# A recurrent cross-attention block with a maxout FFN on one core: another order of the work, single PSUM banks, two batches scored with the states standing, and the last batch's output in fewer pieces

## The chip, the cores and the metric

The kernel runs on one core of a Trainium2 chip. A core has a matrix engine (TensorE, PE in the profile), a vector engine (VectorE, DVE), an activation engine (ScalarE, ACT), a general engine (GpSimd, POOL) and an engine that here only issues transfers (SyncE, SP). Each works through its own list of instructions in order; semaphores hold an instruction back until what it needs is there. The time is device microseconds of the whole program, the median of the runs shown. A profile of one execution gives the span, from its first to its last instruction.

## The reference, cut to what matters

```python
# x: (8, 8, 512, 64), state: (8, 8, 32, 64): batches, heads, tokens, head width
scores  = x @ state.T / 8;   a  = exp(scores - max) / sum      # over the 32 states
scores2 = state @ x.T / 8;   a2 = exp(scores2 - max) / sum     # over the 512 tokens
y = concat([a @ state, a2 @ x], axis=2)                        # 512 + 32 rows per batch and head
# heads side by side: 8 * 544 = 4352 rows of 512
h = max(y @ w1, y @ w2, y @ w3)                                # w: (512, 768)
out = h @ w_out                                                # (4352, 512), float32
```

## The kernel before, in words

The work is in bfloat16 with sums in float32. The kernel doesn't form `a @ state` for the tokens. It multiplies the states of each batch with w1, w2 and w3 first (G, `g_slice` and `g_run`: 64x32 blocks of states as weights, eight of them at a time in the array, since a batch has eight heads), and layer 1 is then one product of the turned weights `aT` with G (`layer1`, L477: six matmuls of 512 columns for each of the six 128-column blocks of the 768). The maximum of three is taken in three steps: ACT copies the first product out of PSUM (`max_first`, L492), VectorE takes the maximum with the second and the third (`max_second` L497, `max_third` L505). Layer 2 is six matmuls into one PSUM bank for each quarter of a batch's tokens (`layer2`, L514); ACT or VectorE copies it out (L526) and a DMA stores it. The 32 state rows of all batches are collected and go through both layers once, at the end (`layer1_states`, `s` in the lists below). The last batch's layer 2 is done in column pieces (`layer2_part` L532, `layer2_part_out` L537, `store_part` L543).

Per batch, ahead of layer 1: the states are cast and turned (`states_cast`, `states_turn` with the matrix engine, four transposes; `states_turn_dma` with a DMA), x is turned (by DMA from batch 2 on), the scores are made (`scores`, L305: 16 matmuls with x as weights and the states' blocks as 64 moving columns), ACT takes the exponential (`exps`, L313), VectorE sums (L342), GpSimd multiplies by the reciprocals (`weights`, L349), and the result is turned by DMA (`a_turn_dma`, L366). `scores_turned`, `exps_turned` and `e_turn_dma`, which stand in the code but not in the order of before, are the other way round: the states' blocks are the weights, x moves, and the exponentials are turned by DMA. The state rows' reading (`sread`, L391) uses the exponentials and x with a column of ones (`pad`).

PSUM has eight banks. Before, four are used singly (tags b0 to b3) and four as two pairs (w0, w1); G and the scores go to pairs, so that one copy takes two banks at once. BANKS, PAIRS and PLACES say which bank or buffer each use takes, in order.

The order of everything is written out by hand: PLAN is a list of short words with arguments, and each word calls one function (`lw 0 2 1`: load columns 0 to 256 of w2; `g 0 1`: G of batch 0, block 1; `l1 3 5`; `l2 2 0`; `so 2 0 2 P`: store from GpSimd's queue). Each engine gets its instructions in the order of that list. In the list of before, batches 3 to 6 repeat one pattern.

The exponentials are taken without subtracting the maximum. `look` takes the largest and smallest of all sums, `flag` (`set_flag`, L575 to L578) makes one number of it with a small matmul and two VectorE instructions, and `vl` (L583) has all five engines read that number. A branch (L674) leads to a second path, which does everything again with the maximum subtracted; with these inputs it is skipped. `hold` puts one matmul and one copy (L591, L593) ahead of the reads. Behind the branch each engine passes some semaphores and a barrier that closes the program (L739).

Of the kernel before, what the change touches and what calls it, by code (L numbers as in the profile page):

```python
# [13 lines left out]
ALU = mybir.AluOpType  # L14
# [4 lines left out]
    lst 0 A; lxu 0 0 S; zero; clr 0; clr 1; clr 2; clr 3; warm; lxg 0 1; busy 1; xones 1; ident; busy 1;  # L19
    lxg 1 0; busy 1; busy 1; stc 0 D; busy 1; busy 1; busy 1; busy 1; busy 1; lxg 1 1; stt 0; busy 1; busy 1;  # L20
    cxu 0 0 D; xt 0 0; stp 0 A; busy 1; xt 0 1; lw 0 2 1; lw 0 1 0; xtc 0 0 D; sc 0 0; xones 0; lw 0 2 2;
    xtc 0 1 D; busy 1; busy 1; sc 0 1; xt 1 0; ex 0 0; ex 0 1; lw 1 3 0; sum 0 0; sum 0 1; xtc 1 0 A; busy 1;
    busy 1; xt 1 1; sc 1 0; xtc 1 1 D; ex 1 0; busy 1; busy 1; sc 1 1; lw 2 3 2; wt 0 1 D; lw 2 3 1; lw 3 4 0;
    wt 0 0 P; lw 3 6 2; at 0 0; sr 0; ex 1 1; sr 1; g 0 0; sum 1 0; wt 1 0 P; g 1 0; atc 0 0 A; at 0 1; at 1 0;
    gc 0 0 A; atc 0 1 A; g 1 1; sum 1 1; gc 1 0 D; atc 1 0 A; srs 0; srs 1; g 0 1; wt 1 1 P; at 1 1; gc 0 1 A;
    l1 0 0; atc 1 1 D; lst 1 A; m0 0 0; lst 3 A; gc 1 1 A; ma 0 0; lw 3 6 1; lw 4 6 0; lxg 2 1; lxg 2 0; l1 0 1;
    m0 0 1; lwo; mb 0 0; g 0 2; g 1 2; ma 0 1; l1 1 0; lst 2 A; gc 0 2 A; mb 0 1; m0 1 0; ma 1 0; l1 0 2;
    mb 1 0; gc 1 2 A; m0 0 2; ma 0 2; l1 1 1; m0 1 1; g 1 3; stc 1 P; mb 0 2; ma 1 1; g 0 3; mb 1 1; stt 1;
    gc 1 3 A; l1 1 2; gc 0 3 A; m0 1 2; stp 1 DA; ma 1 2; g 0 4; g 0 5; l1 0 3; gc 0 5 D; g 1 4; mb 1 2;
    gc 0 4 A; m0 0 3; gc 1 4 A; ma 0 3; gr 2 1792 2304; mb 0 3; l1 1 3; m0 1 3; grc 2 1792 2304 A; xtd 2;  # L30
    ma 1 3; l1 0 5; stc 2 P; g 1 5; gr 2 0 512; mb 1 3; m0 0 5; ma 0 5; l1 1 4; gc 1 5 A; gr 2 1280 1792;
    m0 1 4; grc 2 0 512 D; mb 0 5; gr 2 512 1024; ma 1 4; grc 2 1280 1792 AD; l1 0 4; m0 0 4; ma 0 4; stt 2;
    mb 0 4; sc 2 -; ex 2 -; grc 2 512 1024 D; stp 2 AD; stc 3 D; mb 1 4; l2 0 3; l2 0 0; l2c 0 3 A; l2c 0 0 A;
    sum 2 -; l2 0 1; ones; pad 2; lxg 3 0; lxg 3 1; wt 2 - P; stt 3; xtd 3; l2c 0 1 A; l1 1 5; pad 3;
    so 0 0 2 P; lx 4; m0 1 5; l2 0 2; ma 1 5; mb 1 5; stp 3 A; l2c 0 2 A; l2 1 0; gq 2 1024 1280; gr 3 0 512;
    gr 3 1792 2304; l2c 1 0 D; grc 3 1792 2304 D; gqc 2 1024 1280 A; grc 3 0 512 A; atd 2; sr 2; l2 1 1; srs 2;
    sc 3 -; l1 2 0; m0 2 0; ex 3 -; l2c 1 1 D; l2 1 3; ma 2 0; gq 3 1024 1280; so 0 2 4 P; gqc 3 1024 1280 A;
    l2c 1 3 A; gr 3 512 1024; gr 3 1280 1792; mb 2 0; sum 3 -; wt 3 - P; atd 3; xtd 4; srt 0; sr 3; srs 3;
    l1 2 1; m0 2 1; ma 2 1; l1 2 2; m0 2 2; mb 2 1; ma 2 2; l1 2 3; m0 2 3; mb 2 2; ma 2 3; l1 2 5; m0 2 5;
    mb 2 3; l2 1 2; grc 3 1280 1792 A; grc 3 512 1024 A; ma 2 5; mb 2 5; l2c 1 2 D; l1 2 4; so 1 2 4 P; m0 2 4;  # L40
    ma 2 4; lx 5; mb 2 4; so 1 0 2 P; pad 4; gr 4 1792 2304; gr 4 0 512; grc 4 1792 2304 AD; l2 2 0; l2 2 1;
    grc 4 0 512 D; l2c 2 0 A; l1 3 0; m0 3 0; sc 4 -; ex 4 -; xtd 5; l2c 2 1 D; l2 2 3; ma 3 0; gq 4 1024 1280;
    gr 4 1280 1792; gr 4 512 1024; mb 3 0; sr 4; gqc 4 1024 1280 A; sum 4 -; srs 4; l2c 2 3 A; l1 3 1; m0 3 1;
    ma 3 1; l1 3 2; m0 3 2; mb 3 1; ma 3 2; l1 3 3; m0 3 3; mb 3 2; ma 3 3; l1 3 5; wt 4 - P; m0 3 5; mb 3 3;
    l2 2 2; grc 4 1280 1792 A; grc 4 512 1024 A; ma 3 5; mb 3 5; l2c 2 2 D; l1 3 4; so 2 2 4 P; m0 3 4; ma 3 4;
    lx 6; mb 3 4; atd 4; srt 1; ap 0 A; so 2 0 2 P; pad 5; gr 5 1792 2304; gr 5 0 512; grc 5 1792 2304 AD;
    l2 3 0; l2 3 1; grc 5 0 512 D; l2c 3 0 A; l1 4 0; m0 4 0; sc 5 -; ex 5 -; xtd 6; l2c 3 1 D; l2 3 3; ma 4 0;
    gq 5 1024 1280; gr 5 1280 1792; gr 5 512 1024; mb 4 0; sr 5; gqc 5 1024 1280 A; sum 5 -; srs 5; l2c 3 3 A;
    l1 4 1; m0 4 1; ma 4 1; l1 4 2; m0 4 2; mb 4 1; ma 4 2; l1 4 3; m0 4 3; mb 4 2; ma 4 3; l1 4 5; wt 5 - P;
    m0 4 5; mb 4 3; l2 3 2; grc 5 1280 1792 A; grc 5 512 1024 A; ma 4 5; mb 4 5; l2c 3 2 D; l1 4 4; so 3 2 4 P;  # L50
    m0 4 4; ma 4 4; lx 7; mb 4 4; atd 5; srt 2; ap 1 A; so 3 0 2 P; pad 6; gr 6 1792 2304; gr 6 0 512;
    grc 6 1792 2304 AD; l2 4 0; l2 4 1; grc 6 0 512 D; l2c 4 0 A; l1 5 0; m0 5 0; sc 6 -; ex 6 -; xtd 7;
    l2c 4 1 D; l2 4 3; ma 5 0; gq 6 1024 1280; gr 6 1280 1792; gr 6 512 1024; mb 5 0; sr 6; gqc 6 1024 1280 A;
    sum 6 -; srs 6; l2c 4 3 A; l1 5 1; m0 5 1; ma 5 1; l1 5 2; m0 5 2; mb 5 1; ma 5 2; l1 5 3; m0 5 3; mb 5 2;
    ma 5 3; l1 5 5; wt 6 - P; m0 5 5; mb 5 3; l2 4 2; grc 6 1280 1792 A; grc 6 512 1024 A; ma 5 5; mb 5 5;
    l2c 4 2 D; l1 5 4; so 4 2 4 P; m0 5 4; ma 5 4; mb 5 4; atd 6; srt 3; ap 2 A; so 4 0 2 P; pad 7;
    gr 7 1792 2304; gr 7 0 512; grc 7 1792 2304 AD; l2 5 0; l2 5 1; grc 7 0 512 D; l2c 5 0 A; l1 6 0; m0 6 0;
    sc 7 -; ex 7 -; l2c 5 1 D; l2 5 3; ma 6 0; gq 7 1024 1280; gr 7 1280 1792; gr 7 512 1024; mb 6 0; sr 7;
    gqc 7 1024 1280 A; sum 7 -; srs 7; l2c 5 3 A; l1 6 1; m0 6 1; ma 6 1; l1 6 2; m0 6 2; mb 6 1; ma 6 2;
    l1 6 3; m0 6 3; mb 6 2; srt 4; ma 6 3; l1 6 5; wt 7 - P; m0 6 5; mb 6 3; l2 5 2; grc 7 1280 1792 A;  # L60
    grc 7 512 1024 A; ma 6 5; mb 6 5; l2c 5 2 D; l1 6 4; so 5 2 4 P; m0 6 4; ma 6 4; mb 6 4; atd 7; ap 3 A;
    ap 4 A; so 5 0 2 P; srt 6; l1 7 0; srt 7; m0 7 0; l2 6 0; ap 7 D; srt 5; ma 7 0; mb 7 0; l1 7 2; m0 7 2;
    ap 6 A; l2c 6 0 D; ma 7 2; l1 7 3; m0 7 3; ap 5 A; mb 7 2; ma 7 3; l1 7 4; m0 7 4; l2 6 1; l2c 6 1 A;
    ma 7 4; mb 7 4; l1s 0; m0 s 0; l2 6 2; l2c 6 2 A; look; ma s 0; mb s 0; so 6 2 3 S; mb 7 3; l1 7 1; m0 7 1;
    ma 7 1; l1s 2; m0 s 2; mb 7 1; ma s 2; l1 7 5; m0 7 5; mb s 2; ma 7 5; l1s 1; m0 s 1; ma s 1; so 6 0 1 S;
    mb 7 5; l1s 5; m0 s 5; l2p 7 2 384 512; ma s 5; mb s 1; mb s 5; l1s 3; m0 s 3; l2pc 7 2 384 512 A;
    l2p 7 0 384 512; l2p 7 3 256 512; sop 7 2 384 512 P; ma s 3; l2p 7 2 128 384; mb s 3; l2p 7 0 0 128;
# [38 lines left out]
def kernel(  # L106
# [74 lines left out]
    def bank(shape, dtype, name):  # L181
        return pp.tile(shape, dtype, tag="b" + next(homes["b"]), bufs=1, name=name)
# [491 lines left out]
    with tc.If(bad != 0, label="again"):  # L674
        for b in range(B):
# [11 lines left out]
            if b >= 2:  # L687
                pad(b)
# [55 lines left out]
```

## Time and profile before

| | |
|---|---|
| device time, median of 3 runs | 152.12 us (152.12 to 152.29) |
| span of the profiled execution | 150.5 us |
| granted TensorE clock | 1.000 |
| TensorE busy | 145.1 us, 96% of the span, 1422 matmuls |
| VectorE, ACT, GpSimd busy | 118.0, 83.2, 56.1 us |
| DMA | 22.29 MB, mean 148 GB/s |

The profiled execution has its span; no device time of its own is recorded beside it, so it is set against the runs shown, which are 1.62 us longer at the median. Busy times are unions of instructions that overlap: a 512-column matmul is shown with 379 ns, but six of them follow each other in 1.29 us. Which engine sets the time is therefore read from the chain of work that ended last, and from the idle time ahead of groups of instructions. "L477" is line 477 of the kernel before.

### The profile page before, as it was taken

Reading aid. Unit: us, or ns where it says so; the run is one execution under the profiler, and the core shown is the slowest. Engines: PE = TensorE matmul, PEld = TensorE weight load, DVE = VectorE, ACT = ScalarE, POOL = GpSimd, SP = SyncE. Lnnn points to the kernel's source line nnn. Section 1 sums busy time; section 2 is a strip of 40 time slices with the busy share of each in tenths; the row PEclk is TensorE's granted clock in tenths of the full one; section 3 lists DMA queues with packets and bytes.
Section 4 is the critical chain, followed back from the end, with each engine's and each line's share of the span. In section 5 each row is a group of like instructions: output and inputs, shape, how many; then the busy total and the mean of one; then the engine's idle time right before and its main releaser. Section 6 shows DMA issues by size and latency. Waiting matters only on the chain.

```text
span 150.5 us, 3618 instructions
## 1 busy us (share of the span) xinstructions
PE 145.1 (96%) x1422; PEld 72.8 (48%) x1422; DVE 118.0 (78%) x202; ACT 83.2 (55%) x144; POOL 56.1 (37%) x78
## 2 busy tenths in 40 slices
PE   6998999999999999999999999999999999999991
PEld 2556443335444443444344434443444446689770
DVE  6488788999967899789978997899789888674443
ACT  3366888965654574457546764676466653332220
POOL 6996911090392507350735064506250200001500
PEclk9999999999999999999999999999999999999999
DMA  4999999949647996998399839983303340300555
GB/s 121 195 188 189 206 230 198 196 97 139 124 97 171 235 182 189 108 209 178 145 102 216 183 139 90 231 183 131 157 4 78 121 175 7 139 0 17 190 199 167
DMA packets 39108, 22.29 MB, mean 148 GB/s; under 512 B 23072, under 2 KB 36896, under 8 KB 39088
## 3 DMA queue, kind: packets, MB, share of 16 engines
q0 software_dynamic: 15872, 13.96, 49.3%
q1 hardware_dynamic: 21632, 6.69, 22.8%
q10 hardware_dynamic: 1584, 1.38, 3.2%
q8 instruction: 12, 0.20, 0.6%
q14 instruction: 8, 0.07, 0.2%
HBM read 15.20 MB, written 8.91 MB: 160 GB/s over the span
## 4 chain that ended last, share of the span: by engine, by line
PE 88%; DMA 5%; POOL 3%; issue 1%; DVE 1%; ACT 1%; POOLq 0%
PE pw L477 47%; PE po L514 25%; PE pg L427 6%; DMA w<-in_moe_w_dram 5%; PE po L532 4%; PE ps L305 2%; PE psr L391 2%; POOL w L217 1%; POOL x L206 1%; PE pgh L427 1%; ACT G L444 1%; PE pt L261 1%; DVE held L593 0%; PE idle L591 0%; PE pat L358 0%
## 5 line engine op out<-in xcount | busy, mean ns | idle before, releaser
L477 PE MATMUL pw<-aT,G 128*128 128x512 bf16 x288 | 66.7, 379 | 0.0
L492 ACT CAST t<-pw 128x512 bf16<-128x512 f32 (+1 forms) x54 | 30.5, 564 | 27.3 <-PE pw L477 26.4
L497 DVE TENSOR_TENSOR t<-t,pw 128x512 bf16<-128x512 bf16 (+1 forms) x54 | 35.3, 654 | 11.1 <-ACT t L492 8.9
L477 PEld LDWEIGHTS <-G 128*128 128x128 bf16 x288 | 27.1, 98 | 32.8 <-issue 2.1
L514 PE MATMUL po<-wout,ht 128*128 128x512 bf16 x168 | 39.7, 379 | 0.0
L505 DVE TENSOR_TENSOR ht<-t,pw 128x512 bf16<-128x512 bf16 x48 | 32.9, 686 | 4.5
L349 POOL TENSOR_TENSOR a<-e,rden 128x1024 bf16<-128x1024 bf16 (+1 forms) x9 | 14.6, 1622 | 27.2 <-ACT osb L526 11.1
L514 PEld LDWEIGHTS <-ht 128*128 128x128 bf16 x168 | 15.4, 98 | 19.0 <-issue 1.7
L548 POOL DMA_DIRECT2D out_dram<-osb x13 | 7.4, 571 | 27.5 <-ACT t L492 27.5
L466 ACT CAST G<-pg 128x1024 bf16<-128x1024 f32 (+1 forms) x17 | 14.7, 895 | 2.1 <-PE pg L427 2.1
L526 ACT COPY osb<-po 128x512 f32<-128x512 f32 x15 | 8.9, 592 | 9.1 <-PE po L514 9.1
L526 DVE COPY osb<-po 128x512 f32<-128x512 f32 x14 | 9.6, 688 | 3.9 <-PE po L514 3.8
L375 POOL COPY xp<-x 128x1024 bf16<-128x1024 bf16 x12 | 12.3, 1059 | 0.0
L313 ACT ACTIVATE e<-ps 128x1024 bf16<-128x1024 f32 (+1 forms) x10 | 8.5, 854 | 6.7 <-PE ps L305 6.7
L466 DVE CAST G<-pg 128x1024 bf16<-128x1024 f32 (+1 forms) x12 | 11.6, 995 | 0.0
L342 DVE TENSOR_REDUCE seen<-e 128x32 f32<-128x1024 bf16 (+1 forms) x10 | 10.0, 997 | 1.7 <-ACT e L313 1.7
L427 PE MATMUL pg<-w,bd 64*32 64x512 bf16 (+1 forms) x288 | 10.7, 362 | 0.4 <-DMA w<-in_moe_w_dram 0.2
L444 ACT CAST G<-pg 128x768 bf16<-128x768 f32 x10 | 8.0, 810 | 2.7 <-PE pg L427 2.5
L543 POOL DMA_DIRECT2D out_dram<-osb x4 | 2.2, 544 | 19.4 <-ACT osb L537 19.4
L249 PE MATMUL idle<-zero 128*128 128x512 bf16 x18 | 7.4, 506 | 1.8 <-DVE zero L225 1.3
L477 PE MATMUL pw<-atp,w 128*128 128x256 bf16 x72 | 8.7, 272 | 0.0
L217 POOL DMA_DIRECT2D w<-in_moe_w_dram x10 | 7.7, 782 | 0.0
(70 smaller groups left out, 112.1 us busy)
## 6 DMA issues: line engine op xcount, KB each, us to landing
out_dram<-osb POOLq DMA_DIRECT2D x12, 512.0 KB, 3.7
x<-in_x_dram POOLq DMA_DIRECT2D x4, 512.0 KB, 7.2
x<-in_x_dram POOLq DMA_DIRECT2D x7, 256.0 KB, 5.8
w<-in_moe_w_dram POOLq DMA_DIRECT2D x4, 256.0 KB, 7.5
w<-in_moe_w_dram POOLq DMA_DIRECT2D x2, 384.0 KB, 7.5
wout<-in_moe_w_out_dram POOLq DMA_DIRECT2D x1, 768.0 KB, 12.0
out_dram<-osb SPq DMA_DIRECT2D x3, 256.0 KB, 2.4
stf<-in_state_dram ACTq DMA_DIRECT2D x4, 128.0 KB, 5.3
```

The costliest lines, as they stand in the source:

```text
L342: nc.vector.reduce_sum(out=den, in_=parity(e[b], g), axis=AX.X)
L349: times[c](out=parity(a[b], g).rearrange("p j g s n -> p j (g s) n"), in0=parity(e[b], g).rearrange("p j g s n -> p j (g s) n"), in1=rdens ...
L375: nc.gpsimd.tensor_copy(out=xp[b][:, :, :, g * (D + 1):g * (D + 1) + D], in_=v[:, g])
L427: nc.tensor.matmul(p(s, g), bd(b, 2 * s + g)[64 * g:64 * g + 64, g, :], f(w_sb[64 * g:64 * g + 64, s]), start=True, stop=True, tile_positi ...
L444: copier[c[g]](out=G[b][:, g:h, :, m * 128:m * 128 + 128], in_=p[:, g:h, 0:384].rearrange("p g (i f) -> p g i f", i=3))
L466: copier[c[g]](out=v[:, g:h], in_=p[:, g:h, 0:c1 - c0])
L477: nc.tensor.matmul(pw[i][:, 0:n], lhs(i, k), rhs(k), start=(k == 0), stop=(k == nk - 1))
L492: nc.scalar.copy(out=t0s[b, m][:, 0:n], in_=open_ps["l", b, m][0][:, 0:n])
L497: nc.vector.tensor_max(t1s[b, m][:, 0:n], t0s.pop((b, m))[:, 0:n], open_ps["l", b, m][1][:, 0:n])
L505: nc.vector.tensor_max(ht[b][:, m, :], t1s.pop((b, m))[:, 0:n], open_ps.pop(("l", b, m))[2][:, 0:n])
L514: nc.tensor.matmul(p, ht[b][:, m, tokens(b, j)], wout_sb[:, m, :], start=(m == 0), stop=(m == NM - 1))
L526: copier[c[i]](out=o[:, j, i * w:i * w + w], in_=p[:, i * w:i * w + w])
```

## The change

The list of the order is a new one. What is different in kind:

- PSUM: all eight banks are used singly. G, the scores and the turned scores take two banks of their own, and every copy out of a pair becomes two copies of half the size, which can go to two engines.
- Batches 6 and 7 are scored with the states standing: `scores_turned`, `exps_turned`, `e_turn_dma` in place of `scores` and `exps`.
- The states of batches 4 to 7 (pairs 2 and 3) are turned by DMA, and GpSimd places them.
- The output of the last batch's quarters and of the first half of the state rows comes in eight pieces of 128 to 512 columns; before, in fourteen of 128 or 256.
- The turns of `a` (`atd`) and the loads of x stand elsewhere in the order; weights come in thirteen loads instead of ten.
- `pad` has two columns of ones side by side, and can go to VectorE.
- The flag is made at the end, behind the last output piece.

Three places of the order. First, VectorE's last instructions. Names: `osb` is output on its way to memory, `po` its PSUM, `pst` the flag's product, `nok` and `flag` the number that is read, `hts` the state rows' layer 1. Before:

```order
L537 COPY osb<-po 128x256
L537 COPY osb<-po 128x128
L577 TENSOR_REDUCE nok<-pst 128x1
L578 TENSOR_SCALAR flag<-nok 128x1
L497 TENSOR_TENSOR t_2396<-t_2386,pw_2372 128x256
L505 TENSOR_TENSOR hts<-t_2396,pw_2373 128x256
L526 COPY osb<-po 128x512
L537 COPY osb<-po 128x256 x2
L526 COPY osb<-po 128x512
L537 COPY osb<-po 128x128 x3
L593 CAST held<-idle 128x512
L583 TENSOR_LOAD flag
```

The same place in the changed kernel:

```order
L487 TENSOR_TENSOR t_2427<-t_2373,pw_2338 128x256
L495 TENSOR_TENSOR hts<-t_2427,pw_2339 128x256
L527 COPY osb<-po 128x128
L527 COPY osb<-po 128x512
L527 COPY osb<-po 128x128
L567 TENSOR_REDUCE nok<-pst 128x1
L568 TENSOR_SCALAR flag<-nok 128x1
L583 CAST held<-idle 128x512
L573 TENSOR_LOAD flag
```

The flag stood ahead of two maximum steps and seven copies of output; now it stands behind the last copy. On TensorE its matmul likewise moved behind the last output matmul.

Second, GpSimd's last instructions: stores, the read and the branch (`atp`: the state rows' collected input). Before:

```order
L349 TENSOR_TENSOR a<-e,rden 128x1024
L548 DMA out_dram<-osb 128x1024 x2
L543 DMA out_dram<-osb 128x128 x3
L548 DMA out_dram<-osb 128x512
L543 DMA out_dram<-osb 128x256
L583 TENSOR_LOAD flag
L674 COMPARE_AND_BRANCH
```

In the changed kernel:

```order
L419 COPY atp<-ats 128x4x32
L538 DMA out_dram<-osb 128x1536
L538 DMA out_dram<-osb 128x1024
L538 DMA out_dram<-osb 128x512
L533 DMA out_dram<-osb 128x512
L533 DMA out_dram<-osb 128x128 x2
L573 TENSOR_LOAD flag
L666 COMPARE_AND_BRANCH
```

The read of the flag still follows GpSimd's last store; its stores are now those of batches 4 and 5 and three pieces of the last batch.

Third, ACT at the start, around the first layer-1 block (`e`: exponentials; `aT`: turned weights; G from its PSUM `pg`; `t`: first step of the maximum). Before:

```order
L313 ACTIVATE e<-ps 128x2x2x128 x2
L362 COPY aT<-pat 128x4x128
L444 CAST G<-pg 128x6x128
L362 COPY aT<-pat 128x4x128 x2
L444 CAST G<-pg 128x6x128
L190 DMA stf_75<-in_state_dram 128x256
L492 CAST t_423<-pw_412 128x512
```

In the changed kernel:

```order
L318 ACTIVATE e<-ps 128x2x2x128 x2
L366 COPY aT<-pat 128x4x128
L447 CAST G<-pg 128x3x128 x4
L482 CAST t_433<-pw_424 128x512
L366 COPY aT<-pat 128x4x128
L447 CAST G<-pg 128x3x128 x2
```

A G copy of 768 columns became two of 384, and one turn of `a` moved behind the first step of the maximum.

The diff, with the lists cut to a few lines:

```diff
 PLAN = """
...
-    l2pc 7 0 0 128 A; l2pc 7 3 256 512 D; l2p 7 1 0 128; l2pc 7 0 384 512 D; l2p 7 3 0 256; flag;
...
+    1280 1792 AD; l2c 2 1 A; sq 6; gr 6 1280 1792; sq 7; eq 7; l1 4 5; m0 4 5; grc 6 1280 1792 DA; pad 6 P; l1 4
...
-    l2pc 7 1 384 512 D; sop 7 1 384 512 A; l2pc 7 0 128 256 D; sop 7 0 128 256 A; sos 1 S; sop s 0 0 256 S;
-    sop 7 0 256 384 S; hold; vl;
+    A; sop 7 3 0 512 P; sop 7 0 0 128 P; sop 7 1 0 384 S; sop 7 0 128 256 S; sop 7 0 256 512 A; sop 7 1 384 512
+    P; flag; hold; vl;
 """
...
     def bank(shape, dtype, name):
-        return pp.tile(shape, dtype, tag="b" + next(homes["b"]), bufs=1, name=name)
-
-    def two_banks(shape, dtype, name):
-        return pp.tile(shape, dtype, tag="w" + next(homes["w"]), bufs=1, name=name)
+        return pp.tile(shape, dtype, tag="b" + next(homes[0]), bufs=1, name=name)
...
     def scores(b, g=None):
+        if g is None:
+            ps = [bank([128, 2, 2, HS, Ns], F32, "ps") for _ in range(2)]
+        else:
+            p = bank([128, J, 1, HS, Ns], F32, "ps")
+            ps = [p[:, 2 * i:2 * i + 2] for i in range(2)]
...
     def scores_turned(b):
-        p = open_ps["sq", b] = two_banks([128, 2, 2, 2, 128], F32, "pst")
+        ps = open_ps["sq", b] = [bank([128, 2, 2, 128], F32, "pst") for _ in range(2)]
         for g in range(2):
             for s in range(HS):
                 for c in range(2):
                     nc.tensor.matmul(
-                        p[32 * s:32 * s + 32, c, :, g, :], bd(b, 2 * s + g)[64 * c:64 * c + 64, c, :],
+                        ps[c][32 * s:32 * s + 32, :, g, :], bd(b, 2 * s + g)[64 * c:64 * c + 64, c, :],
                         xT[b][64 * c:64 * c + 64, 2 * s + g, :, :],
...
     def exps_turned(b):
         new(eT, b, [128, 2 * J * 128], "eT")
-        nc.scalar.activation(
-            out=eT[b], in_=open_ps.pop(("sq", b)).rearrange("q c i g t -> q (c i g t)"), func=AF.Exp, scale=scale)
+        for c, p in enumerate(open_ps.pop(("sq", b))):
+            nc.scalar.activation(
+                out=eT[b][:, c * 512:c * 512 + 512], in_=p.rearrange("q i g t -> q (i g t)"), func=AF.Exp, scale=scale)
...
-    def pad(b):
+    def pad(b, c="P"):
         new(xp, b, [128, HS, J, 2 * D + 2], "xp")
-        nc.gpsimd.memset(xp[b][:, :, :, D:D + 1], 1.0)
+        {"D": nc.vector, "P": nc.gpsimd, "A": nc.gpsimd}[c].memset(xp[b][:, :, :, D:D + 2], 1.0)
...
     def g_slice(b, m):
-        p = open_ps["g", b, m] = two_banks([128, 2, 512], F32, "pg")
+        ps = open_ps["g", b, m] = [bank([128, 512], F32, "pg") for _ in range(2)]
...
     def g_ran(b, c0, c1, c):
         new_g(b)
-        p, ps = open_ps.pop(("g", b, c0))
...
+        v = G[b].rearrange("p g i f -> p g (i f)")
+        for g, p in enumerate(open_ps.pop(("g", b, c0))):
+            copier[c[g % len(c)]](out=v[:, g, c0:c1], in_=p[:, 0:c1 - c0])
```

The second path, which is skipped, is written with single banks in the same way.

233 lines of the change are left out of this document (108 added, 125 removed), and 4 rows, old and new, of the table BANKS.

## The prediction

> **What bounds the kernel now.** First the head of the page, with the busy times and the shares of the chain of work that ended last:
>
> ```profile
> span 150.5 us, 3618 instructions
> PE 145.1 (96%) x1422; PEld 72.8 (48%) x1422; DVE 118.0 (78%) x202; ACT 83.2 (55%) x144; POOL 56.1 (37%) x78
> PE 88%; DMA 5%; POOL 3%; issue 1%; DVE 1%; ACT 1%; POOLq 0%
> ```
>
> The chain lies on TensorE for 88% of the span. So I read the same chain in order of time (start, length, what), to see where it is not on TensorE:
>
> ```profile
> 6.06 7.41 DMA w<-in_moe_w_dram
> 13.47 0.14 issue
> 13.60 0.40 PE pg L427 x8
> 14.00 0.02 issue
> 14.02 0.81 ACT G L444
> 14.83 0.04 issue
> 14.88 0.68 PE pg L427 x16
> 15.55 0.33 PE pat L358 x4
> 15.88 2.59 PE pw L477 x12
> ...
> 34.06 0.22 PE pt L261 x4
> ...
> 57.19 0.56 PE pg L427 x16
> ...
> 61.74 0.47 PE ps L305 x16
> 62.20 1.29 PE po L514 x6
> 63.50 0.23 PE pgh L427 x8
> 63.73 0.43 PE pg L427 x16
> ...
> 135.09 0.33 PE po L532 x6
> ...
> 144.29 2.67 PE po L532 x36
> 146.95 0.02 issue
> 146.98 0.30 DVE osb L537
> ```
>
> Three stages. Until 15.88 the kernel waits for x and the first columns of w1 to w3, then for one copy out of PSUM. From 15.88 to 146.95, 131.07 us, the chain never leaves TensorE: there only less TensorE work, or a new wait, changes the time. Call its last matmul T. The last 3.55 us (150.5 - 146.95) are the end: copy, stores, the read of the flag by every engine, the branch past the safe path and the closing barrier. The page shows the end least, so I asked for the instructions of the lines of the read (L583), the branch (L674) and the closing (L739), stretch by stretch, and for the timeline and DMA landings there (rows: engine, operation, durations in ns, first and last start):
>
> ```profile
> 139.78 0.16 DVE L577 TENSOR_REDUCE nok<-pst 128x1 f32<-128x2 f32 x1 [1.39 <-PE pst L575]
> 139.98 0.15 DVE L578 TENSOR_SCALAR flag<-nok 128x1 int32<-128x1 f32 x1
> L583 POOLq TENSOR_LOAD <-flag x1: 795/795/795, 140.7 to 140.7; - x1
> 140.91 0.54 POOL L543 DMA_DIRECT2D out_dram<-osb  x1
> out_dram<-osb POOLq DMA_DIRECT2D x1, 128.0 KB, 4.3
> L674 POOLq COMPARE_BRANCH  x1: 70/70/70, 141.6 to 141.6; - x1
> L674 POOLq EVENT_SEMAPHORE  x5: 17/42/43, 142.1 to 145.3; - x5
> L674 POOLq INC_SWDGE_SEM  x1: 967/967/967, 145.4 to 145.4; - x1
> L739 POOLq DRAIN  x1: 3247/3247/3247, 146.4 to 146.4; - x1
> L739 SPq DRAIN  x1: 7/7/7, 149.4 to 149.4; - x1
> L739 POOLq EVENT_SEMAPHORE  x2: 17/17/17, 149.7 to 149.7; - x2
> L739 ACTq EVENT_SEMAPHORE  x1: 17/17/17, 149.8 to 149.8; - x1
> ```
>
> GpSimd has the longest way out. It reads the flag at 140.7, branches at 141.6, waits at five semaphores (its store of 140.91 lands 4.3 us later, at 145.2, and the last semaphore is at 145.3), adjusts its DMA semaphores (0.97 us), and drains for 3.25 us, to 149.65. Its barrier semaphores at 149.7 come next, and 0.1 us later the other engines are released (149.8). SyncE had been there at 149.4. So GpSimd is already the last, by a quarter of a microsecond; it can be that near only because the flag is written at 140.13, before TensorE's last 6.8 us.
>
> **The change, part by part.** All sums are against the profiled span; the runs shown lie 1.62 us above it (152.12 - 150.5), which I keep.
>
> *Start.* Before, the second pair of G slices waits for a two-bank PSUM tile that ACT's 0.81 us copy must free (14.02 to 14.83), then come four transposes, then the first layer-1 matmul at 15.88. With eight single banks those slices don't wait. What is left is the w load at 13.47 (the same 640 columns have to be in) and now two copies of half the size behind each other. From the rows below, a 384-column half lies between 0.375 us (256) and 0.586 us (512), so about 0.48, and two end at 14.02 + 0.96 = 14.98. Layer 1 could start 0.9 us earlier; one set of four transposes (0.22 us) now comes behind it. Taken: -0.7. Bounds: -0.9, and 0 if the next column block of w3, needed before layer 1 in the new order, is late.
>
> *TensorE's work.* The states of batches 4 to 7 are turned by DMA: two sets of four transposes fall away, 2 x 0.22 = -0.44. Fewer pieces: six matmuls of 128 columns take 0.33, so a 512-column output in four quarters 1.32 against 1.29 whole; some five quarters and five halves fewer save about 0.05. Scores with the states standing: 32 matmuls of 64 columns, x as weights, become 32 of 256 columns with the states' 64x32 blocks as weights. The nearest row, eight 64x32 matmuls of 256 columns in 0.23 us, is 29 ns each, and the old form is 0.47/16 = 29 ns each as well: -0.02 for both batches, nothing. The Trainium skill, "TensorE: Matmul & The Clock Gate", Part 3, "Measured speedup vs the span model", has packed tiles follow each other by some 4 ns, so that sixteen of them would take little longer than one; by it both batches together would save about a quarter of a microsecond. Here the eight took 29 ns each, and I stay with the row. Sum: -0.5.
>
> *Single banks.* Each two-bank copy becomes two. From the groups by line, shapes kept apart (busy us, mean ns):
>
> ```profile
> L466 ACT CAST G<-pg 128x1024 bf16<-128x1024 f32 x12 | 11.7, 1024 | 0.0
> L444 ACT CAST G<-pg 128x768 bf16<-128x768 f32 x10 | 8.0, 810 | 2.7 <-PE pg L427 2.5
> L466 ACT CAST G<-pg 128x512 bf16<-128x512 f32 x5 | 2.9, 586 | 2.1 <-PE pg L427 2.1
> L469 ACT CAST G<-pgh 128x256 bf16<-128x256 f32 x12 | 3.9, 375 | 3.8 <-PE pgh L427 3.8
> ```
>
> A split costs 2 x 0.586 - 1.024 = 0.15 us. ACT's G copies were 11.7 + 8.0 + 2.9 + 3.9 = 26.5 us; by the new order they are 36 of 512, 19 of 384 and 6 of 256 columns, 21.1 + 9.1 + 2.3 = 32.5. With eight more output copies moved to it, ACT comes to some 94 us, and VectorE, which gives those up, to some 112: both well under TensorE. The cover is TensorE's 131 us; where copies bunch (G of batches 6 and 7 beside two output copies, some 3.5 us on ACT) it is gone for a moment. Bounds for the 131 us as a whole: -0.65, if the five stretches like 57.19 (0.56) came down to 0.43; +1.5, about one layer-1 block, if TensorE waits for banks. Taken: 0, since no wait shows in the chain now and eight banks give more room than four and two pairs.
>
> *DMA.* Two turns of states and two of exponentials join SyncE's queue, loads of x come earlier, turns of `a` elsewhere. SyncE issues in order: behind `atd` 4, which waits for GpSimd's `wt` 4, stand a store, the turn of the last states and the turns of x for 7 and 6, and for those wait the standing scores. All are issued several layer-1 blocks (1.29 us each) before they are read, so I cost them at 0; without that cover each late turn is one of the waits in the +1.5.
>
> *The end.* This is the large term. The flag's matmul, `nok` and `flag` now stand behind the last output copy. VectorE's last copy takes T + 0.03 to T + 0.33 (row at 146.98), `nok` and `flag` 0.35 more (139.78 to 140.13): T + 0.7. GpSimd's way then runs after T: 0.9 from read to branch (140.7 to 141.6), 0.5 to the first semaphore, 0.3 for five that wait for nothing, 1.0 for the adjustment (145.4 to 146.4), 3.25 drain, and 0.85 from the drain's end to the end of the span. 0.7 + 0.9 + 0.5 + 0.3 + 1.0 + 3.25 + 0.85 = 7.5 us, against 3.55: +3.95. The bounds: +0.85 if the drain costs only 0.1 us when nothing is outstanding; below that 0, if everything behind the flag were hidden. GpSimd's last stores wait for nothing late, and the last store of all leaves ACT near T + 0.1; even with 4.3 us it lands ahead of GpSimd's end.
>
> Sum: T = 146.95 - 0.7 - 0.5 = 145.75, span 145.75 + 7.5 = 153.25, time 153.25 + 1.62 = **154.9 us**, slower by 1.8%.
>
> **Rivals.**
>
> *The drain is a wait.* Its end follows SyncE's last drain (149.4) by only 0.25 us, as if it had waited for the others. Then the end is 4.4 us after T: 145.75 + 4.4 + 1.62 = 151.8. Against it: these rows do not hold waiting time, for the five semaphores last 17 to 43 ns each though 3.2 us pass from the first to the last. The Trainium skill, "Perfetto Trace Analysis", section "Sequencer-only Instruction (DRAIN, etc)", says the same: the profiled window is the execution, behind the semaphore wait. By that rule the drain is 3.25 us of work, and the time is that of the forecast. 0.25.
>
> *The end costs nothing, the change is faster.* One mechanism: GpSimd's drain and adjustment run beside the other engines' reads and the last landings, so the end stays 3.55 us. 145.75 + 3.55 + 1.62 = 150.9. For it: today most of GpSimd's way is hidden. Against: a read cannot come before the flag, and the rows behind the read add up to more than 3.55. 0.08.
>
> *TensorE waits.* The order is no longer the same in each batch, and copies bunch; with the upper bound of 1.5 us and a short drain, 153.3. Against it: VectorE's work falls. It decides from 0.3 us of waits on. 0.12.
>
> **How the numbers follow.** Forecast 0.55, its own range 154.2 to 156.6 (start 0 instead of -0.7, and waits up to 1.0 beside it). What a measurement of this kernel can tell from no change is about 0.2%, 0.3 us. Faster: the second rival's 0.08 and somewhat under half of the first's 0.25, together 0.19. Same: about a third of the first, 0.09. Slower: the rest, 0.72. The range must reach to the first rival: 151.3 to 156.5.
>
> **What would show it.** Right: GpSimd's read of the flag starts about 0.7 us after TensorE's last output matmul, its drain is again near 3.2 us, and the other engines are released some 6.7 us after T. The first layer-1 matmul starts near 15.2, four sets of transposes of states are two, and TensorE's stretch is near 130.6 us. Wrong: a drain of about 0.1 us, or a release at about T + 2.9; on the other side, VectorE or ACT as releasers of TensorE in the waits, for more than a microsecond in all.

## The result, and the profile after

| | before | after |
|---|---|---|
| device time, median of 18 runs each | 152.14 us (151.56 to 153.55) | 153.34 us (152.45 to 154.15) |
| ratio, 95% interval | | 1.0083 (1.0063 to 1.0103) |
| span of the profiled execution | 150.5 us | 151.6 us |
| TensorE's last output matmul ends (T) | 146.96 us | 146.75 us |
| from T to the end of the span | 3.54 us | 4.85 us |

The change makes the kernel slower by 0.8%; 1.8% were forecast. The direction and the range held, the size didn't. The head of the changed kernel's page, with the shares of the chain that ended last:

```profile
span 151.6 us, 3522 instructions
PE 143.9 (95%) x1367; PEld 70.0 (46%) x1382; DVE 110.5 (73%) x203; ACT 85.4 (56%) x170; POOL 59.4 (39%) x80
PE 81%; DVE 6%; DMA 5%; POOL 3%; issue 2%; ACT 1%; POOLq 0%
```

TensorE's share of the chain fell from 88% to 81%, and VectorE, which had 1%, has 6%. The chain in order of time shows where:

```profile
5.99 7.73 DMA w<-in_moe_w_dram
...
13.86 0.43 PE pg L431 x8
...
14.32 0.40 PE pat L362 x4
14.72 0.61 PE pg L431 x24
15.33 0.39 PE pat L362 x4
15.72 1.29 PE pw L467 x6
...
38.01 1.09 ACT e L315 x2
...
39.13 1.23 DVE seen L346
...
41.38 2.47 DVE xp L379 x2
...
47.68 5.18 PE pw L467 x24
...
83.20 0.34 PE pst L326 x16
83.54 0.22 PE pg L431 x8
83.76 0.22 PE pst L326 x16
```

The start is almost where it was (15.72 against 15.88). From 39 to 45 us the chain is on VectorE: two copies of x into `xp` (the pad of batch 2, which the kernel before gave to GpSimd) stand ahead of copies out of PSUM that TensorE waits for. The scores with the states standing are the two rows of 0.34 and 0.22 us near 83 us.

The end, from the timeline of VectorE and the instructions of the lines of the read (L573), the branch (L666) and the closing (L730):

```profile
147.17 0.15 DVE L568 TENSOR_SCALAR flag<-nok 128x1 int32<-128x1 f32 x1
L573 POOLq TENSOR_LOAD <-flag x1: 809/809/809, 147.4 to 147.4; - x1
L666 POOLq COMPARE_BRANCH  x1: 70/70/70, 148.2 to 148.2; - x1
L666 POOLq INC_SWDGE_SEM  x1: 451/451/451, 149.2 to 149.2; - x1
L730 POOLq DRAIN  x3: 46/109/1124, 149.7 to 151.4; - x3
L730 SPq EVENT_SEMAPHORE  x14: 17/28/28, 149.6 to 151.6; - x14
L730 SPq DRAIN  x3: 7/7/12, 150.3 to 151.1; - x3
L730 ACTq EVENT_SEMAPHORE  x2: 17/17/17, 151.0 to 151.6; - x2
```

The flag is indeed last and GpSimd's read comes 0.7 us after T, as forecast. But GpSimd's adjustment of its DMA semaphores (INC_SWDGE_SEM) takes 0.45 us and not 0.97, and its drain 1.12 us and not 3.25. SyncE's closing semaphores start as the adjustment ends (149.65), and the others are released at 151.0.

### The profile page after: what moved, and what is told of

Read it like the earlier page. It is cut to its first block, busy times and chain, and to the rows that moved or that the text cites. A ratio compares the mean times of both kernels' runs of the same rounds, so it can differ in the third digit from the quotient of the medians.

```text
span 151.6 us, 3522 instructions
## 1 busy us (share of the span) xinstructions
PE 143.9 (95%) x1367; PEld 70.0 (46%) x1382; DVE 110.5 (73%) x203; ACT 85.4 (56%) x170; POOL 59.4 (39%) x80
## 4 chain that ended last, share of the span: by engine, by line
PE 81%; DVE 6%; DMA 5%; POOL 3%; issue 2%; ACT 1%; POOLq 0%
PE pw L467 46%; PE po L504 20%; PE pg L431 6%; DMA w<-in_moe_w_dram 5%; PE po L522 4%; DVE xp L379 2%; PE ps L303 1%; PE psr L395 1%; POOL w L210 1%; POOL x L199 1%; DVE t L487 1%; DVE G L459 1%; DVE seen L346 1%; ACT e L315 1%; PE pat L362 1%
## 5 line engine op out<-in xcount | busy, mean ns | idle before, releaser
L495 DVE TENSOR_TENSOR ht<-t,pw 128x512 bf16<-128x512 bf16 x48 | 32.0, 683 | 2.4
L459 ACT CAST G<-pg 128x512 bf16<-128x512 f32 (+1 forms) x42 | 21.4, 569 | 6.8 <-PE pg L431 6.8
L516 ACT COPY osb<-po 128x512 f32<-128x512 f32 x21 | 12.5, 602 | 8.1 <-PE po L504 4.4
L538 POOL DMA_DIRECT2D out_dram<-osb x9 | 5.0, 564 | 29.5 <-issue 17.6
L431 PE MATMUL pg<-w,bd 64*32 64x512 bf16 (+2 forms) x336 | 12.2, 350 | 0.6 <-DMA w<-in_moe_w_dram 0.4
L459 DVE CAST G<-pg 128x512 bf16<-128x512 f32 (+1 forms) x18 | 10.2, 587 | 2.1 <-PE pg L431 2.0
L379 POOL COPY xp<-x 128x1024 bf16<-128x1024 bf16 x10 | 10.1, 1041 | 0.1
L447 ACT CAST G<-pg 128x384 bf16<-128x384 f32 x19 | 8.3, 490 | 2.9 <-PE pg L431 2.6
L467 PEld LDWEIGHTS <-w 128*128 128x128 bf16 x72 | 7.0, 98 | 1.5
L431 PEld LDWEIGHTS <-bd 64*32 64x32 bf16 x336 | 3.5, 89 | 8.5 <-issue 7.6
L516 DVE COPY osb<-po 128x512 f32<-128x512 f32 x8 | 5.5, 685 | 2.1 <-PE po L504 2.1
```

The costliest lines, as they stand in the source:

```text
L379: copier[c](out=xp[b][:, :, :, g * (D + 2):g * (D + 2) + D], in_=v[:, g])
L431: nc.tensor.matmul(p(s, g), bd(b, 2 * s + g)[64 * g:64 * g + 64, g, :], f(w_sb[64 * g:64 * g + 64, s]), start=True, stop=True, tile_positi ...
L459: copier[c[g % len(c)]](out=v[:, g, c0:c1], in_=p[:, 0:c1 - c0])
L467: nc.tensor.matmul(pw[i][:, 0:n], lhs(i, k), rhs(k), start=(k == 0), stop=(k == nk - 1))
L495: nc.vector.tensor_max(ht[b][:, m, :], t1s.pop((b, m))[:, 0:n], open_ps.pop(("l", b, m))[2][:, 0:n])
L516: copier[c[i]](out=o[:, j, i * w:i * w + w], in_=p[:, i * w:i * w + w])
```

## The experiments

All runs, with the first layer-1 matmul and TensorE's stretch from there to T by TensorE's timeline (which shows a matmul from its read on, some 0.16 us ahead of the chain), and the end from T on:

| run | first layer-1 | stretch | end | ratio to before (95%) |
|---|---|---|---|---|
| before | 15.72 | 131.24 | 3.54 | 1 |
| after | 15.55 | 131.20 | 4.85 | 1.0083 (1.0063 to 1.0103) |
| e1, flag early | 15.79 | 131.44 | 4.97 | 1.0091 (1.0057 to 1.0125) |
| e2, pad on GpSimd | 15.45 | 131.56 | 4.89 | 1.0090 (1.0061 to 1.0119) |
| e3, both | 15.62 | 131.45 | 5.13 | 1.0123 (1.0083 to 1.0162) |
| e4, before with late flag | 15.71 | 131.20 | 7.39 | 1.0250 (1.0217 to 1.0283) |
| e5, flag early, branch held | 16.03 | 130.96 | 3.81 | 1.0043 (1.0026 to 1.0061) |
| e6, two more stores | 15.39 | 130.90 | 5.11 | 1.0093 (1.0068 to 1.0118) |
| e7, pad on GpSimd, x earlier | 15.32 | 134.85 | 4.93 | 1.0236 (1.0199 to 1.0274) |
| e8, e5 and e7 | 16.08 | 132.79 | 3.83 | 1.0129 (1.0102 to 1.0156) |
| e9, e4 with four more stores | 15.40 | 131.23 | 4.67 | 1.0081 (1.0053 to 1.0109) |
| e10, waits out | 15.22 | 131.04 | 3.84 | 1.0032 (1.0006 to 1.0058) |
| e11, before, states by DMA | 15.44 | 131.06 | 3.70 | 1.0037 (1.0014 to 1.0059) |
| e12, before, copies split | 15.66 | 131.51 | 3.23 | 1.0024 (1.0007 to 1.0041) |
| e13, one more wait out | 15.52 | 130.99 | 3.79 | 1.0009 (0.9989 to 1.0028) |
| e14, after, scores as before | 15.33 | 132.03 | 4.84 | 1.0115 (1.0095 to 1.0135) |
| e18, e13 with banks swapped | 15.49 | 131.85 | 3.86 | 1.0088 (1.0067 to 1.0109) |

The columns of times are of one trace each, the ratio is of several executions. Three more runs are one execution each: e15 and e16 are second traces of e10 and e11, and e17 was run for its trace.

### The place of the flag: e4, e1, e5

Theory: the flag's late place makes the longer end. Rival: the larger last stores make it. e4 is the kernel before with the flag late:

```diff
-  l2p 7 3 0 256; flag; l2pc 7 1 0 128 A
+  l2p 7 3 0 256; l2pc 7 1 0 128 A
-  sop 7 0 256 384 S; hold; vl;
+  sop 7 0 256 384 S; flag; hold; vl;
```

> The kernel before, with the flag's three instructions put behind the last output piece, as the change has them; nothing else moved. Theory 1 (the flag's late place alone makes the longer end): the end goes from 3.55 us after T to about 4.9, ratio 1.0085. Theory 2 (the pieces and stores make it): the end grows by at most 0.4 us, ratio at most 1.003. By the prediction's sum, with GpSimd's drain fixed at 3.25 us, it would be 7.5 us after T, ratio 1.026.

Measured 1.025, an end of 7.39 us. GpSimd and SyncE at its end:

```profile
L674 POOLq INC_SWDGE_SEM  x1: 967/967/967, 149.2 to 149.2; - x1
L739 POOLq DRAIN  x3: 46/109/3247, 150.2 to 154.1; - x3
L739 SPq EVENT_SEMAPHORE  x14: 17/28/28, 150.2 to 154.3; - x14
```

This is the prediction's sum come true, in the kernel before: 7.5 us were worked out, with the adjustment of 0.97 and the drain of 3.25 us behind the branch. Both are as long here as where they were hidden. The theory that the late flag alone costs what it costs in the changed kernel was 2.5 us short: besides the place of the flag, the length of two GpSimd instructions decides.

e1 is the change with the flag early:

```diff
-  l2pc 7 0 0 128 D; l2p 7 1 384 512
+  l2pc 7 0 0 128 D; flag; l2p 7 1 384 512
-  sop 7 1 384 512 P; flag; hold; vl;
+  sop 7 1 384 512 P; hold; vl;
```

> The changed kernel, with the flag's matmul, sum and comparison put behind the copy of the first 128-column piece, some 6 us ahead of TensorE's last output matmul (T); nothing else moved. Theory 1 (the flag's late place makes the longer end): GpSimd's way out runs beside the last pieces again and the end falls from 4.86 us after T to about 3.6, 1.2 us less, so that the ratio to the kernel before is about 1.000. Theory 2 (the later and larger last stores hold SyncE's closing drain, the flag costs only the 0.4 us between SyncE's last drain and the release): the end falls by no more than 0.4 us, to about 4.5, and the ratio is about 1.0055.

Neither: 1.0091, an end of 4.97 us. GpSimd is done early (drain from 146.4 on), but the last stores land late. From the timeline of SyncE, the instructions of the branch, and the DMA view from 147 to 148 us:

```profile
147.57 1.28 SPq L533 DMA_DIRECT2D out_dram<-osb  x1
L666 PEldq COMPARE_BRANCH  x1: 479/479/479, 145.9 to 145.9; - x1
q8 instruction: 1, 0.02, 7.8%
out_dram<-osb SPq DMA_DIRECT2D x1, 64.0 KB, 3.3
```

SyncE's last store takes 1.28 us to issue, 0.36 us in the changed kernel, and lands 3.3 us after its issue began, 2.2 there. With the flag early, TensorE's sequencer reads it and branches at 145.9, ahead of T, and a transfer on the queue q8, which the page calls instruction, runs among the last stores; I take it for a load of the code behind the branch. In the changed kernel it runs after 150 us. The list has a word against this: `hold` puts a matmul ahead of the read, in a PSUM bank. In the kernel before it is the bank of VectorE's last output copy, so the branch waits for that copy; in the changed list it is a bank that has long been free, and only the late flag held the branch. e5 gives it the last piece's bank:

```diff
-  hold   (bank 5)
+  hold   (bank 1, that of l2p 7 0 128 256)
```

> The changed kernel with the flag early as in the first run of this study, and the PSUM bank of the last matmul before the branch (L581) changed from 5 to 1, the bank of the last output piece, so that TensorE does not reach its read of the flag before VectorE's last copy. Theory 1 (in the first run TensorE's branch at 145.9, 1.3 us ahead of T, sent its load of new code into the last stores, which landed 1.2 us later): branch at 148 or later, SyncE's last store is issued in 0.36 us instead of 1.28 and lands in about 2.2 us, the end falls from 4.97 us after T to about 3.6 and the ratio to the kernel before is about 1.000. Theory 2 (the larger last stores land late by themselves): the end stays above 4.5 us and the ratio above 1.006.

```profile
L666 PEldq COMPARE_BRANCH  x1: 479/479/479, 148.2 to 148.2; - x1
out_dram<-osb SPq DMA_DIRECT2D x1, 64.0 KB, 2.2
```

The end falls to 3.81 us, and the ratio to 1.0043. So of the 1.31 us that the end grew in the traces, 1.04 are the late flag and 0.27 what is left with it early: the last stores are larger, and SyncE's last drain ahead of the release comes at 149.9, 2.9 us after T, against 2.4 before. By the ratios the gain is smaller, 0.4% or 0.6 us, and their intervals allow 0.2 to 1.0. That holding the branch cures the stores is shown; that the transfer on q8 is what delays them is only read from the times that agree: with the branch held it runs after 149 us, when the stores are all but done.

### What GpSimd's last two instructions count: e6, e9, e17

The adjustment and the drain keep their length wherever the flag stands, and to the nanosecond in every run that leaves GpSimd's transfers alone (e11 and e12 beside e4; e2, e7 and e14 beside e1 and e5). But they differ between the two kernels: 0.97 and 3.25 us, 0.45 and 1.12. So they may follow what was put through GpSimd's queue. e6 tests the number of transfers and splits two of the change's stores:

```diff
-  so 2 2 4 P        -  so 4 0 2 P
+  so 2 2 3 P; so 2 3 4 P        +  so 4 0 1 P; so 4 1 2 P
```

> The changed kernel, flag late as it has it, with two of GpSimd's earlier stores (batch 2, tokens 2 to 3, and batch 4, tokens 0 to 1) split in two each: 39 DMAs on GpSimd's queue instead of 37, as many as the kernel before has; the same bytes. Theory 1 (the 0.97 us adjustment and the 3.25 us drain of the kernel before follow the number of DMAs on this queue): both come back here, the end is about 7.5 us after T and the ratio 1.025. Theory 2 (they follow something else in the program): 0.45 and 1.12 us as in the changed kernel, and the ratio stays near 1.008.

```profile
L666 POOLq INC_SWDGE_SEM  x1: 491/491/491, 148.7 to 148.7; - x1
L730 POOLq DRAIN  x3: 46/109/1287, 149.3 to 151.1; - x3
```

Neither theory: the number of DMAs is now that of the kernel before (39), and the times grew by 40 and 163 ns only, 20 and 82 for each split. The kernel before lies 26 such steps higher (516 and 2123 ns). The next theory was that they count the rows of all transfers, in a list that is used over and over (the expectation calls an entry a descriptor and the list a ring; no run shows the list itself), and follow how far it is filled at the end. If that count wraps, four more splits there should bring it down. e9 is e4 with four stores split in the same way (`so 4 0 2`, `so 4 2 4`, `so 5 0 2`, `so 5 2 4`):

> The kernel before with the flag late (as in the fourth run of this study), and four of GpSimd's stores (both halves of batches 4 and 5) split in two each: 512 descriptors more on GpSimd's queue, the same bytes, 43 DMAs. Theory 1 (the time of GpSimd's adjustment and drain follows how far its descriptor ring of 256 entries for each of the 16 engines is filled: 16 in the changed kernel with 0.45 and 1.12 us, 32 with two more stores, 0.49 and 1.29, and 224 in the kernel before, 0.97 and 3.25; a straight line through all three): 32 entries more wrap the ring to 0, the adjustment takes about 0.41 us and the drain 0.96, the end falls from 7.4 us after T to about 4.6 and the ratio from 1.025 to about 1.007. Theory 2 (both grow with each descriptor or DMA added): 1.05 and 3.6 us, ratio about 1.028. Theory 3 (both belong to the program as a whole): 0.97 and 3.25 us, ratio 1.025.

```profile
L674 POOLq INC_SWDGE_SEM  x1: 407/407/407, 149.0 to 149.0; - x1
L739 POOLq DRAIN  x3: 46/109/961, 149.5 to 151.0; - x3
```

0.41 and 0.96 us were worked out, 0.407 and 0.961 came, and the late flag, which cost 2.5% in e4, costs 0.8% here with more stores to issue. So the length behaves like a count that starts again from a low value: 26 steps above the changed kernel and four more come out at two below it, a period of 32 splits. What it counts is not settled. Each split added a DMA and, by the shape of the stores, 128 rows, and the period of 32 splits fits by itself; the ring of 256 that was written down is one reading of it. Counted by the rows of all transfers on this queue, over 16 engines, the changed kernel stands at 16 of 256, as written, but the kernel before at 216 and not at 224, one step of 8 too low; by rows alone four splits would not yet have wrapped. e17 (each of the four whole loads of x as two halves, `lxg b 0; lxg b 1` for `lx b`) adds DMAs without rows:

> The changed kernel with the four whole loads of x (batches 4 to 7) made as two loads of half the heads each: four DMAs more on GpSimd's queue, the same number of descriptors (8 heads by 128 partitions), where the two runs with split stores had added 128 descriptors with each DMA. Theory 1 (GpSimd's adjustment and drain at the end follow the filling with data descriptors): 0.45 and 1.12 us, as in the changed kernel. Theory 2 (each DMA adds 82 ns to the drain and 20 ns to the adjustment, whatever it holds): 0.53 and 1.45 us. The time says little here, since the loads themselves change.

```profile
L666 POOLq INC_SWDGE_SEM  x1: 471/471/471, 148.6 to 148.6; - x1
L730 POOLq DRAIN  x3: 46/109/1206, 149.1 to 150.9; - x3
```

One step for four DMAs, where the one theory had none and the other four. Both the rows and the DMAs themselves seem to count, in steps; no run parts them further. The packets that the traces count on this queue don't help: they grow by 16 for each added DMA in e6, e9 and e17 alike.

### The waits of TensorE: e2, e3, e7, e8, e10, e15, e13, e18

e2 gives the pad of batch 2 back to GpSimd (`pad 2 D` to `pad 2 P`), e3 is e1 and e2 together.

> The changed kernel with the two copies of x for batch 2 (2.6 us on VectorE) given to GpSimd, as they were before; nothing else moved. Theory 1 (these copies hold VectorE's G and output copies, and so TensorE, between 34 and 48 us): the 1.3 us of waits there fall to about 0.3, T comes 1.0 us earlier, the ratio to the kernel before falls from 1.0083 to about 1.002. Theory 2 (the waits come from the order of this stretch and from the copies split in two, and VectorE's other work fills the place): T moves by less than 0.3 us, ratio 1.006 to 1.009.

> The changed kernel with both edits, the early flag and the copies of x for batch 2 on GpSimd. If both first theories hold the gains add: 1.0083 less 0.8% less 0.65% is about 0.994 of the kernel before, faster than it. If only the flag's holds, about 1.000; if only the copies' holds, about 1.000 too, and the places in the trace tell which (T near 145.7 or an end of 3.6 us).

Both ratios stay up (1.0090 and 1.0123). In e2 the wait near 45 us is gone: the scores of batch 4 start 44.19 us after the first layer-1 matmul instead of 45.05. So it was worth 0.9 us. But the next wait takes it back. The wait of TensorE in e2, and its chain at that place:

```profile
PE ps L303 <- DMA xT<-x: 1.2, 1, 1.2
55.95 6.82 DMA xT<-x
```

The turn of x for batch 5 lands at 62.8 us here, and the scores of batch 5 wait for it. In the changed kernel it landed at about the same time, 62.5 us, and the wait on VectorE had covered it. e7 moved the loads of x for batches 4 and 5 behind those of batch 3 and a turn ahead on SyncE, and e8 added the end of e5.

> The changed kernel with the copies of x for batch 2 on GpSimd, the loads of x for batches 4 and 5 right behind those of batch 3, and the turn of x for batch 4 ahead of the turn of a for batch 3 on SyncE's queue. Theory 1 (with VectorE's copies gone the next wait of TensorE was for the turn of x for batches 4 and 5, near 61 us, and it hid the gain of 1.0 us): both waits go, T comes to about 145.5 and the ratio falls from 1.0083 to about 1.000. Theory 2 (a third wait takes the place): T stays above 146.4 and the ratio above 1.006.

> The changed kernel with both sets of edits: the flag early with the branch held, the copies of x on GpSimd, the loads and the turn of x earlier. If both first theories hold, T is near 145.5, the end 3.6 us, the span 149.1, and the ratio to the kernel before about 0.992. If only the one on the end holds, about 1.000; if neither, about 1.008.

That was worse than what it mended (1.0236 and 1.0129). From e7, its longest wait of TensorE, the piece of the chain that covers it, and the stretch behind it (us, busy time of PE, PEld, DVE, ACT and POOL, then the granted clock, DMA share, GB/s):

```profile
PE ps L303 <- DMA xT<-x: 2.2, 1, 2.2
44.31 4.99 DMA aT<-a
50.00:55.00 5.00, 5.00 (x17) 1.93 (x16) 3.02 (x5) 2.85 (x6) 3.01 (x3) 0.68 0.41 78
```

The earlier loads ran beside the turns of x for batches 2 and 3, whose issue on SyncE took 16.7 us instead of 12.9. TensorE stood still from about 46.3 to 48.5 us for the turn of x for batch 3, made those scores, and then waited 0.3 us more for the turn of `a` behind it in the queue, which came late as well. Its clock was granted at 0.68 in the 5 us from 50 on. e10 leaves the loads alone and puts the scores of batch 5 one output block later (`l2 2 0; sc 5 -; ex 5 -`), with pad on GpSimd and the end of e5:

> The changed kernel with the flag early, the branch held by the last piece's bank, the copies of x for batch 2 on GpSimd, and the scores of batch 5 one output block later (behind that of batch 2, token block 0), the loads and turns of x where the change has them. Theory 1 (TensorE's two waits, VectorE's copies at 38 to 45 us and the turn of x for batch 5 at 61 us, are each alone on their path, and the early flag gives the short end): T near 145.8, end 3.8 us, span 149.6, ratio to the kernel before 0.994 to 0.998. Theory 2 (another wait takes their place again): T stays near 147, ratio 1.004 as with the early and held flag alone.

T is 146.26 and the span 150.1 us, 0.4 under the kernel before, but over its 12 executions the ratio is 1.0032: they lie from 151.9 to 153.7 us. A second trace of the same kernel (e15) is of one at 153.7:

> The tenth run's kernel once more, for a second trace: its executions lie at 151.9 to 152.3 and at 152.7 to 153.7 us, and the trace at hand is of the faster sort. Theory 1 (the loads at the start arrive at different times): a slow execution has its first layer-1 matmul later than 15.2 us, and the same stretch. Theory 2 (a transfer in the middle comes late in some executions): the same start and a longer stretch, with a wait for a DMA in it.

```profile
5.99 8.56 DMA w<-in_moe_w_dram
...
56.93 7.33 DMA xT<-x
```

Both theories hold half: the first columns of the weights land 0.94 us later than in the other trace (7.62 us there), and the stretch is 0.9 us longer, with the wait for the turn of x in it. In the faster trace G of batch 4 waited for a bank that the exponentials held (`62.96 1.09 ACT e L315 x2` in its chain); e13 moved the two G blocks ahead, and e18 then swapped two banks:

> The tenth run's kernel with its last wait of TensorE taken out: at 62.9 us the G columns of batch 4 wait 1.07 us for a bank that the exponentials of batch 5 hold. Here the two G column blocks come ahead of the output block and of those scores, with banks that nothing late holds, and the copies of both go to ScalarE. Theory 1 (the work saved on TensorE, some 0.9 us, shows once no wait is left): the stretch from the first layer-1 matmul to T falls from 131.0 to about 130.0 us, the ratio to the kernel before is 0.992 to 0.998. Theory 2 (the stretch is held by something that these profiles do not name as a wait): it stays near 131, ratio 1.000 to 1.005.

> The thirteenth run's kernel with the PSUM banks of one layer-1 block (batch 3, columns 4) in the order 2, 1, 3 instead of 2, 3, 1, since its second bank was the one that ScalarE's late output copy held, at 64.3 to 65.0 us. Theory 1: the wait of some 0.4 us goes, T comes that much earlier, ratio to the kernel before 0.997 to 0.999. Theory 2 (the next thing is late by as much): ratio 1.001 as before this edit.

e13 reaches the time of the kernel before (1.0009), with 130.99 us of stretch; e18 loses again (1.0088). It put bank 3 last in the layer-1 block, where the third step of the maximum (L495) reads it late, and the second output block behind it needs bank 3:

```profile
PE po L504 <- DVE ht L495: 1.2, 1, 1.2
```

Each wait taken out near 40 to 70 us was followed by another of about its size. None of these orders beats the kernel before.

### Parts of the change alone: e14, e11, e12

e14 is the change with the scores of batches 6 and 7 as before (`sc`, `ex` for `sq`, `eq`, `etd`).

> The changed kernel with the scores of batches 6 and 7 as the kernel before has them (x as weights, 32 matmuls of 64 columns for each batch, no turn of the exponentials by DMA), at the same places. Theory 1 (the rows of the changed kernel's trace: 0.47 us for a batch in the old form, 0.28 in the new): TensorE works 0.38 us more, ratio 1.0105 against 1.0083. Theory 2 (the prediction: both forms cost 29 ns a matmul, 0.02 us apart): ratio unchanged, rows of 0.47 us in both forms.

```profile
83.32 0.47 PE ps L303 x16
```

The old form, 16 matmuls a batch (the 32 of the expectation are both batches'), costs 0.47 us for a batch, the new one 0.34 and 0.22; the ratio goes from 1.0083 to 1.0115. The intervals overlap, but rows and medians (0.8 us apart) agree on the sign: the standing form is worth about the 0.38 us of its rows. Of the 0.83 us by which the stretch of this trace is longer, 0.5 come at these rows; the other 0.3 are there before them, where the two lists are the same.

e11 is the kernel before with `std 2`, `std 3` for `stt 2`, `stt 3`, and e12 the kernel before with each two-bank copy and exponential as two:

> The kernel before with one part of the change alone: the states of batches 4 to 7 turned by DMA, at the places where TensorE turned them. Theory 1 (the prediction's term): eight transposes fewer on TensorE, T 0.44 us earlier, ratio 0.997. Theory 2 (SyncE's queue and the DMA engines are full there, and the turns of x for batches 2 and 3 come late in turn): T the same or later, ratio 1.000 to 1.005.

> The kernel before with every copy and exponential over two PSUM banks made as two over one bank each, on the engine it had; banks, order and all else as they were. Theory 1 (the prediction: 0.15 us more for each on ACT or VectorE, hidden under TensorE): T within 0.2 us of 146.95, ratio 1.000 to 1.002. Theory 2 (the pairs of banks come free later and TensorE waits, up to one layer-1 block): T up to 1.5 us later, ratio up to 1.010.

e11 comes out at 1.0037, although its traces (two of them) have a stretch 0.2 us shorter and spans of 150.2 and 150.6; its executions lie from 151.9 to 153.5 us, and no trace of one above 153 was taken. Where those lose a microsecond stays open. So of the 0.44 us forecast for these transposes 0.2 reached the stretch, and the time did not fall. e12 costs 0.24%, some 0.4 us (0.1 to 0.6 by its interval), and its stretch is 0.27 us longer: a split copy is not quite hidden.

## Why the prediction was right and wrong, by its steps

*The end, +3.95.* This is the step that failed, in two terms: "1.0 for the adjustment (145.4 to 146.4), 3.25 drain". The path was right: read at T + 0.7, branch, semaphores, adjustment, drain, release. Put 0.45 and 1.12 us in place of these two durations and the prediction's 7.5 us becomes 4.82; 4.85 were measured. e4 shows the sum right for the program that the durations were read from. What failed is to carry the length of two GpSimd instructions from one program to another as if it belonged to the instruction; it belongs to what that program had put through GpSimd's queue. The lower bound (a drain of 0.1 us) was on record, but it stood for a drain with nothing outstanding, and that is not what shortened it: in all these traces GpSimd's own stores have landed before the drain begins.

*The rival "the drain is a wait"* is as far off as the forecast (151.8 and 154.9 against 153.3). Its end of 4.4 us is much nearer to the 4.85 than the forecast's 7.5, but that is luck, since its mechanism is refuted. In e5 the drain takes 1124 ns from 146.7 on, with stores of SyncE still to come, and the same 1124 ns at 149.7 in the changed kernel; in e4 it takes 3247 ns to 153.4 although SyncE's last drain ahead of the release came at 150.9. So it does not wait for the others. The Trainium skill, "Perfetto Trace Analysis", section "Sequencer-only Instruction (DRAIN, etc)", has the profiled window begin when the semaphores are satisfied and hold the execution alone, and these rows agree.

*The end costs nothing*: refuted by e5 and e4.

*The start, -0.7.* Measured -0.16 in the two traces. Over the kernels that keep the start of before (six traces: before, e4, e9, e11 and its second trace, e12) the first layer-1 matmul is at 15.40 to 16.02, on average 15.66 us; over the fourteen with the start of the change at 15.05 to 16.16, on average 15.57. The wait for the two-bank tile did go, but it was smaller than the prediction read it. ACT's copy takes 0.81 us in the chain before, yet TensorE's timeline has eight transposes in that time and stands idle for 0.20 us only:

```profile
14.05 0.62 PE L358 MATMUL pat<-ident,a 128*128 128x128 bf16 x8
14.88 0.68 PE L427 MATMUL pg<-w,bd 64*32 64x384 bf16 x16 [0.20 <-ACT G L444]
```

The prediction let the copies alone decide when layer 1 can start (14.98). In the changed kernel TensorE has 32 G matmuls and eight transposes of its own between the landing of the weights and layer 1 (13.86 to 15.72, the chain on TensorE all the way); before there were 32 and twelve (13.60 to 15.88). That is 0.42 us less, the 0.20 of the wait and four transposes that now come behind layer 1's start, by which T gains nothing. And the weights landed 0.25 us later in this trace (13.72 against 13.47). The landing itself scatters by a microsecond.

*TensorE's work, -0.5.* The states' part was too large (0.2 of 0.44 in e11's stretch), the scores' part too small: the standing scores came to 0.56 us for both batches instead of 0.94, where the prediction had 29 ns for each matmul and no gain. The row it leaned on was one of eight matmuls (0.23 us); sixteen in a row take 0.22 to 0.34. The Trainium skill, "TensorE: Matmul & The Clock Gate", Part 3, "Measured speedup vs the span model", has packed tiles follow each other by some 4 ns, from which the prediction estimated a gain of about a quarter of a microsecond for both. Worked again, eight in 0.23 us and eight more at 4 ns each are an estimate of 0.26 for a batch and a gain of 0.4 for both. The rows give 0.38, so either estimate was nearer than the 29 ns that were chosen over it.

*Single banks, 0.* Mis-sized: splitting alone costs about 0.4 us in the kernel before (e12), and the new order has a wait of 0.9 us near 45 us. The upper bound of 1.5 stood for such waits and held; but the wait comes from VectorE, which the prediction had relieved, through the pad that it took over from GpSimd. *Rival "TensorE waits"*: 153.3 by its sum, with the waits (0.9) and the short drain both there in part; its time is nearest to what was measured, but by other amounts, so that too is luck.

Together: in the two traces the stretch from the first layer-1 matmul to T is the same within 0.1 us, work saved and waits added about equal; the rest is the end. The end was forecast 2.65 us too long, the start and the stretch together 1.0 us too short, so the forecast is 1.6 us off only because its errors partly cancel.

## What to carry to other kernels

What closes a program on an engine may have a length that the program itself sets; before such a length is put on the path, look whether it is the same in another program, or keep the work hidden by giving its release (here, the flag) early. When an instruction is moved early, look at what its lateness had held back: here a branch of TensorE, and with the branch early the last stores came late. And a wait taken out of a tight order is worth only as much as the slack of the next thing that was late behind it.

## What the runs showed of the hardware that was not expected

GpSimd's adjustment of DMA semaphores behind a skipped branch took 407 to 967 ns and its closing drain 961 to 3247 ns, in fixed proportion (20 to 82 ns a step), the same to the nanosecond wherever they stood in time, and four more stores on its queue made them shorter by 0.56 and 2.29 us. With TensorE's branch taken 1.3 us ahead of the end of its last output matmul, three stores of other engines took 1.1 to 1.2 us longer (192, 128 and 64 KB: 3.3, 3.4 and 3.3 us against 2.1, 2.2 and 2.2), and one DMA issue 1.28 us instead of 0.36; with the branch held they did not.
